# Ranks of the attention over three engines' later steps, and the first expert's gather above the jump

## The chip, the cores and the metric

One core of a Trainium2 chip runs the program. Its engines are TensorE (PE, with its weight loads as PEld), VectorE (DVE), ScalarE (ACT), GpSimd (POOL) and SyncE (SP), which issues most of the DMAs; POOL issues the indirect ones. Each engine has its own instruction queue and works in order; semaphores join them. Matrix products accumulate in PSUM, all else lies in SBUF. The metric is the device time of one execution in microseconds (us), as a median of several runs.

## The reference

Three stages stand one behind the other, on 3072 tokens of width 384. Cut to what is computed:

```python
def _attn_ref(r, k, v, w, u):                     # 4 batches, 8 heads, 768 tokens, 48 wide
    for t in range(S):
        cur = np.einsum('bhd,bhe->bhde', u[None] * kt, vt)
        y[:, :, t] = np.einsum('bhd,bhde->bhe', rt, state + cur)
        state = w[None, :, :, None] * state + np.einsum('bhd,bhe->bhde', kt, vt)

def _moe_ref(x, w_gate, w1, w2):                  # 8 experts, 384 -> 1024 -> 384
    logits = x @ w_gate
    expert_idx = np.argmax(logits, axis=1)        # one expert for each token
    probs = np.exp(logits - logits.max(-1, keepdims=True))
    probs /= probs.sum(-1, keepdims=True) + 1e-09
    for e in range(E):
        mask = expert_idx == e
        ye = np.maximum(x[mask] @ w1[e], 0.0) @ w2[e]
        out[mask] = gate_w[mask, None] * ye       # gate_w: the chosen expert's probs

def _moe2_ref(x, w_in, w_out):                    # 384 -> 2048 -> 384
    h = x @ w_in
    return (h - np.tanh(h)) @ w_out
```

## The kernel before, in words

**Attention** (to about 145 us). The sequence is cut into chunks of 128 tokens, six for each of the four batches: 24 steps, chunk by chunk, so that four steps belong to one chunk. The loop over `n` in `manual_schedule` writes the work of all engines in one order by hand, and every engine takes its part of it in that order. Around step `n`, SP loads the input of step `n + 3` (`load`, tiles n and t), POOL makes rk, rku, kh (L318, L324, L333, the keys and receptances scaled for a coming step) and sw (L382, the state decayed), DVE makes dt (L338), t (L313), am (L360) and Sc (L383), ACT makes am's diagonal (L345), copies y (L413) and the state Sb (L395), and PE the products between. Seven steps late, `xout_t` (L541) turns the output round through PE, `xout_g` scales it by the gate on ACT (xs, L548) and SP stores it in DRAM (xd, L550); the SP queue holds that store ahead of the load that follows it.

**Gate and ranks.** `at_step(n, first, fn)` calls `fn(c)` for chunk `c` at the step that lies `first` behind the chunk's start, counted so that it falls on one step in four. `logits`, `logits2`, `gate` find the expert of each token (OH, one-hot), `rank_mm` counts on PE how many earlier tokens went there. `rank_sel` (L483 on) makes of it the token's rank (RK), the tile hs and the row lo within the tile, by comparing with thr, and from them one-hot arrays: `ohh` (L495) and `ol` (L511) on DVE, `hv` (L500) and the tile part of `rh` (L504) on POOL, and the row part of `rh` (L509) on ACT, for the chunk before the last on POOL (L507). `idx_mm` (L520) multiplies `ol` by `rh` on PE, and the sum over chunks (`idf`, L529) is the list of tokens sorted by expert. All of `rank_sel` stands in one step, the *rank step*, and `idx_mm` in the next.

**Head and jump.** The first 256 tokens of expert 0 can be known after four chunks; their product with that expert's weights, the *head* (`head1`, `head2` for f from 0 to 7, nine matmuls each), fills PE around the end of the attention. `EARLY` of the head2 stand before the jump `tc.If(fr > 0)` (L837), whose body is skipped here and redoes the head in another case. Behind the jump, the casting of the list (L856) and `first_gather` (two indirect DMAs of 128 rows, L595) fetch the other tokens of the first block; `first_trans(kk)` for kk from 0 to 2 turns them on PE (L601), ACT casts (L602) and DVE subtracts (L603). The small DVE operations of `order()` are handed out between the heads as `steps`.

**Experts** (159 to 380 us): 64 blocks, eight for each expert. In block `i` the kernel runs `mm1(i)` (L1043) and `mm2(i)` (L1068). `gather(e + 2)` stands at the sixth block of expert e: three or four indirect DMAs (L1019) on POOL; `xg_trans` turns them three to five blocks of the next expert on. `refill` loads weights by SP (L76) and splits them on ACT (L84) and on DVE or POOL (L85). **Second FFN** (380 us to the end): `nm1` and `nm2` (L1295, L1343).

Of the kernel before, what the change touches and what calls it, by code (L numbers as in the profile page):

```python
# [30 lines left out]
def rwkv_moe_moe_kernel(ctx: ExitStack, tc: tile.TileContext, rk_t, rkv, pk, u, wp1, wp2, out):  # L31


    nc = tc.nc
# [382 lines left out]
    e8p, s4p = sm[:, 32:32 + E], sm[:, 32 + E:32 + 2 * E]  # L417
    scp = sm[:, 64:64 + B * E].rearrange("p (b e) -> p b e", e=E)
# [64 lines left out]
    def rank_sel(c):  # L483
        rk = sm[:, 192:192 + 8 * B].rearrange("p (b e) -> p b e", e=E)
        pr = gp.tile([P, B, E], F32, tag="pr", name="pr")
        nc.vector.tensor_tensor(out=pr, in0=rk, in1=OH[:, c], op=ALU.mult)
        rank = RK[:, c]
        nc.vector.tensor_reduce(out=rank, in_=pr, axis=AX.X, op=ALU.add)
        ge = gp.tile([P, B, 4], F32, tag="ge", name="ge")
        nc.vector.tensor_tensor(out=ge, in0=bc(rank.unsqueeze(2), [P, B, 4]),  # L490
                                in1=thr.unsqueeze(1).to_broadcast([P, B, 4]), op=ALU.is_ge)
        hs = gp.tile([P, B], F32, tag="hs", name="hs")
        nc.vector.tensor_reduce(out=hs, in_=ge, axis=AX.X, op=ALU.add)
        ohh = gp.tile([P, B, 4], F16, tag="ohh", name="ohh")
        nc.vector.tensor_tensor(out=ohh, in0=bc(hs.unsqueeze(2), [P, B, 4]),  # L495
                                in1=q1.unsqueeze(1).to_broadcast([P, B, 4]), op=ALU.is_equal)
        lo = gp.tile([P, B], F32, tag="lo", name="lo")
        nc.vector.scalar_tensor_tensor(out=lo, in0=hs, scalar=float(-P), in1=rank, op0=ALU.mult, op1=ALU.add)
# [11 lines left out]
        ol = gp.tile([P, B, P], F16, tag="ol", name="ol")  # L510
        nc.vector.tensor_tensor(out=ol, in0=iotaf.unsqueeze(1).to_broadcast([P, B, P]), in1=bc(lo.unsqueeze(2), [P, B, P]),  # L511
                                op=ALU.is_equal)
        st["ol", c], st["rh", c] = ol, rh
# [109 lines left out]
    def by_token():  # L623

        with tc.tile_pool(name="slow", bufs=1) as sp:
# [10 lines left out]
            for c in range(C):  # L636
# [33 lines left out]
                rank_sel(c)  # L670
                idx_mm(c)
# [4 lines left out]
    with tc.manual_schedule():  # L676
# [39 lines left out]
        LAG = 7  # L716
        LOADS = {1: (0, 0), 3: (0, 1), 5: (1, 0), 7: (1, 1), 9: (2, 0), 11: (2, 1), NN - 1: (3, 0)}
# [3 lines left out]
        for n in range(NN + 1):  # L721
# [54 lines left out]
            if n < NN:  # L776
                at_step(n, 5, idx_mm)
# [17 lines left out]
        L = C - 1  # L795
        EARLY = 2
# [17 lines left out]
        logits(L)  # L814
        xout_t(NN - 6)
# [15 lines left out]
        rank_sel(L)  # L831
        head1(1)
        head1(2)
        idx_mm(L)
        for f in range(EARLY):
            head2(f)
        with tc.If(fr > 0, label="slow"):  # L837
# [85 lines left out]
        for f in range(CH1):  # L923
# [7 lines left out]
            if 0 <= f - (CH1 - 3 - KD) < KD:  # L931
                first_trans(f - (CH1 - 3 - KD))
# [269 lines left out]
    with tc.manual_schedule():  # L1202
# [8 lines left out]
        for i in range(NC1):  # L1211
# [19 lines left out]
            if f == CH1 - 3 and e + 2 < E:  # L1231
                gather(e + 2)
# [228 lines left out]
```

## Time and profile before

| what | us |
|---|---|
| median of 3 runs (lowest, highest) | 792.38 (791.72, 793.81) |
| the profiled execution's own time | 790.21 |
| its span, first to last instruction | 786.5 |
| PE busy | 763.5 (97%) |
| PE's weight loads busy | 696.9 (89%) |
| DVE busy | 637.8 (81%) |
| ACT busy | 524.7 (67%) |
| POOL busy | 450.8 (57%) |

The mean granted clock of TensorE is 0.997 of full speed. Busy times are averages over three very different stages, and each stage has to be read by itself: the windows cut the span, the timeline lists the instructions of an engine in order with the idle time ahead of each and what ended it, and the waits add such times up by line.

### The profile page before, as it was taken

How to read it: one execution, taken by the hardware profiler on the slowest of the kernel's cores; microseconds unless marked ns; L12 is line 12 of the kernel's file. 1: busy time of each engine (PE TensorE's matmuls, PEld its weight loads, DVE VectorE, ACT ScalarE, POOL GpSimd, SP SyncE). 2: the span in 40 equal slices, each digit the busy share in tenths (PEclk: the TensorE clock that was granted, in tenths of full speed). 3: DMA queues.
4: the chain of work that ended last, by engine and by line, in shares of the span. 5: the costliest groups of instructions: out<-in, count | busy, mean ns of one | idle time of the engine just before them, and what ended most of it. 6: DMA issues, size and time to landing. Idle time of an engine off the chain costs nothing.

```text
span 786.5 us, 14413 instructions
## 1 busy us (share of the span) xinstructions
PE 763.5 (97%) x5052; PEld 696.9 (89%) x5052; DVE 637.8 (81%) x1124; ACT 524.7 (67%) x1135; POOL 450.8 (57%) x438
## 2 busy tenths in 40 slices
PE   7799999999999999999999999999999999999997
PEld 7578887898899989999899889989989988998887
DVE  6799888678798868994598888888888888888893
ACT  8789888454545545545687777777776677777871
POOL 6999995257668668665265443534435354353533
PEclk9999999999999999999999999999999999999999
DMA  7989973267798979974200000000001000000100
GB/s 216 261 234 281 249 241 115 86 193 233 200 241 257 276 233 280 261 241 134 80 1 1 1 30 11 2 11 31 0 2 41 1 0 21 21 1 0 42 1 40
DMA packets 34972, 89.82 MB, mean 114 GB/s; under 512 B 5690, under 2 KB 13022, under 8 KB 34896
## 3 DMA queue, kind: packets, MB, share of 16 engines
q1 hardware_dynamic: 30704, 78.87, 34.4%
q0 software_dynamic: 4192, 9.99, 4.3%
q8 instruction: 41, 0.67, 0.4%
q14 instruction: 35, 0.29, 0.1%
HBM read 73.10 MB, written 15.74 MB: 113 GB/s over the span
## 4 chain that ended last, share of the span: by engine, by line
PE 50%; issue 2%; ACT 1%; POOL 1%; POOLq 0%
PE h L1295 25%; PE o L1343 23%; PE y L1068 1%; PE hps L1043 1%; POOL out_dram L1356 0%; PE o L1295 0%; POOL g L1332 0%; POOLq L1402 0%; POOL xb L1332 0%; ACT mk L1305 0%; ACT s L1303 0%; POOLq L1456 0%; ACT xb L1331 0%; ACT z L1299 0%; ACT t L1301 0%
## 5 line engine op out<-in xcount | busy, mean ns | idle before, releaser
L1332 POOL TENSOR_TENSOR g<-t,g 128x512 fp32r<-128x512 f32 x93 | 120.3, 1294 | 178.2 <-ACT g L1331 126.7
L1295 PE MATMUL h<-xb,ring 128*128 128x512 f32 x855 | 213.6, 395 | 0.0
L1343 PE MATMUL o<-ring,g 128*128 128x384 f32 x1116 | 209.4, 336 | 0.0
L1343 PEld LDWEIGHTS o<-ring,g 128*128 128x128 f32 x1116 | 196.1, 188 | 8.2
L1295 PEld LDWEIGHTS h<-xb,ring 128*128 128x128 f32 x855 | 159.7, 188 | 30.5
L85 POOL TENSOR_TENSOR ring<-stg,ring 128x384 fp32r<-128x384 f32 x102 | 104.5, 1049 | 55.7 <-ACT ring L84 48.3
L1299 ACT ACTIVATE z<-h 128x512 f32<-128x512 f32 x95 | 56.9, 599 | 96.5 <-PE h L1295 96.5
L1068 PE MATMUL y<-h,ring 128*128 128x256 f32 (+7 forms) x576 | 114.0, 342 | 0.0
L1043 PE MATMUL hps<-xt,ring 128*128 128x472 f32 (+6 forms) x504 | 105.8, 354 | 1.4 <-DVE h L1047 1.3
L1068 PEld LDWEIGHTS y<-h,ring 128*128 128x128 f32 x576 | 101.4, 188 | 3.2
L1311 DVE TENSOR_TENSOR t<-t,h 128x512 f32<-128x512 f32 x95 | 65.0, 684 | 41.8 <-ACT t L1301 41.5
L1043 PEld LDWEIGHTS hps<-xt,ring 128*128 128x128 f32 x504 | 90.5, 188 | 5.4 <-DVE h L1047 1.4
L84 ACT CAST ring<-stg 128x384 fp32r<-128x384 f32 x152 | 70.4, 513 | 18.7 <-DMA stg<-in_wp_dram 18.2
L1316 DVE COPY_PREDICATED t<-mk,h 128x512 f32<-128x512 uint32 x95 | 71.5, 752 | 10.5 <-DVE h L1314 0.9
L1313 DVE SCALAR_TENSOR_TENSOR h<-s,h 128x512 f32<-128x512 f32 x95 | 66.2, 696 | 9.9
L1046 ACT ACTIVATE h<-hps 128x256 fp32r<-128x256 f32 (+7 forms) x64 | 32.0, 501 | 56.9 <-PE hps L1043 56.6
L1303 ACT ACTIVATE s<-z,gb 128x512 f32<-128x512 f32 x96 | 69.6, 725 | 0.0
L1305 ACT ACTIVATE mk<-z,gt 128x512 f32<-128x512 f32 x96 | 69.3, 722 | 0.0
L1314 DVE SCALAR_TENSOR_TENSOR h<-z,h 128x512 f32<-128x512 f32 x95 | 66.1, 696 | 3.3
L1312 DVE TENSOR_TENSOR h<-h,z 128x512 f32<-128x512 f32 x95 | 65.8, 692 | 0.0
L1331 ACT CAST g<-t 128x512 fp32r<-128x512 f32 x93 | 57.6, 619 | 8.5 <-DVE t L1316 6.4
L345 ACT ACTIVATE am<-ident,dt 128x128 f32<-128x128 f32 x192 | 58.6, 390 | 3.1 <-DVE dt L338 3.0
(246 smaller groups left out, 1095.2 us busy)
## 6 DMA issues: line engine op xcount, KB each, us to landing
stg<-in_wp_dram SPq DMA_DIRECT2D x64, 384.0 KB, 4.9
n<-in_rkv_dram SPq DMA_DIRECT2D x24, 576.0 KB, 7.2
d<-in_wp_dram SPq DMA_DIRECT2D x32, 384.0 KB, 6.0
t<-in_rk_t_dram SPq DMA_DIRECT2D x48, 192.0 KB, 7.5
wdec<-dcf SPq DMA_DIRECT2D x32, 192.0 KB, 5.5
xd<-xs SPq DMA_DIRECT2D x24, 192.0 KB, 3.1
stg<-wdec SPq DMA_DIRECT2D x12, 384.0 KB, 4.1
wl<-wdec SPq DMA_DIRECT2D x2, 768.0 KB, 5.1
```

The costliest lines, as they stand in the source:

```text
L84: nc.scalar.copy(out=dst[:, 0, sl], in_=of)
L85: eng.tensor_tensor(out=dst[:, 1, sl], in0=of, in1=dst[:, 0, sl].bitcast(F32), op=ALU.subtract)
L1043: nc.tensor.matmul(ps, lhsT=wf(a, kk), rhs=xt[e][b][:, kk, :], start=(n == 0), stop=(n == 8))
L1068: nc.tensor.matmul(yps[d], lhsT=wf(a)[:, d * P:(d + 1) * P], rhs=h2[:, b, :], start=(f == 0 and n == 0), stop=(f == CH1 - 1 and n == 2))
L1295: nc.tensor.matmul(ps, lhsT=wf(a, kk), rhs=xb[j][:, b, kk, :], start=(n == 0), stop=(n == 8))
L1303: nc.scalar.activation(out=s, in_=z, func=ACTF.Square, scale=G_K ** 0.5, bias=gb)
L1305: nc.scalar.activation(out=mk, in_=z, func=ACTF.Relu, scale=-1.0, bias=gt2)
L1313: nc.vector.scalar_tensor_tensor(out=ps, in0=s, scalar=G_K * G_D, in1=ps, op0=ALU.add, op1=ALU.mult)
L1314: nc.vector.scalar_tensor_tensor(out=ps, in0=z, scalar=G_A, in1=ps, op0=ALU.subtract, op1=ALU.mult)
L1316: nc.vector.copy_predicated(out=t, mask=mk.bitcast(U32), data=ps)
L1332: nc.gpsimd.tensor_tensor(out=g[:, 1, :], in0=ww, in1=g[:, 0, :].bitcast(F32), op=ALU.subtract)
L1343: nc.tensor.matmul(ops[q], lhsT=gg[i][:, b, q * P:(q + 1) * P], rhs=wf(a), start=(f == 0 and n == 0), stop=(f == CH2 - 1 and n == 2))
```

## The change

It moves work between steps, and three small arrays to another memory:

- `rank_sel` is cut in pieces. `rank_of` (rank, ge, hs) stays in the rank step; `rank_in` (lo, ohh, ol) comes one step later; `rank_q` (hv and the tile part of rh, on POOL), `rank_row` (the row part, now on ACT for every chunk) and `idx_mm` come one step after that. What needs the list for the head comes one step later with it.
- thr is copied to PSUM (thp), and hs and lo are made there (hsp, lop).
- `first`, the cast of the list and the first gather, stands above the jump and in the skipped body; EARLY is 1, not 2; `first_trans` stands at f = 4, 5, 6, not 2, 3, 4.
- `gather(e + 2)` is spread over three blocks: two parts at f = 5, one at 6, one at 7.

```diff
+    thp, hsp, lop = sm[:, 48:52], sm[:, 52:56], sm[:, 56:60]
...
     def rank_sel(c):
+        rank_of(c)
+        rank_in(c)
+
+    def rank_of(c):
...
-                                in1=thr.unsqueeze(1).to_broadcast([P, B, 4]), op=ALU.is_ge)
-        hs = gp.tile([P, B], F32, tag="hs", name="hs")
-        nc.vector.tensor_reduce(out=hs, in_=ge, axis=AX.X, op=ALU.add)
+                                in1=thp.unsqueeze(1).to_broadcast([P, B, 4]), op=ALU.is_ge)
+        nc.vector.tensor_reduce(out=hsp, in_=ge, axis=AX.X, op=ALU.add)
+
+    def rank_in(c):
+        nc.vector.scalar_tensor_tensor(out=lop, in0=hsp, scalar=float(-P), in1=RK[:, c], op0=ALU.mult, op1=ALU.add)
...
+        nc.vector.tensor_tensor(out=ol, in0=iotaf.unsqueeze(1).to_broadcast([P, B, P]),
+                                in1=bc(lop.unsqueeze(2), [P, B, P]), op=ALU.is_equal)
+    def rank_q(c):
...
-        if c == C - 2:
-            nc.gpsimd.tensor_scalar(out=rh[:, :, 1, :], in0=hv, scalar1=pid, scalar2=None, op0=ALU.mult)
-        else:
-            nc.scalar.activation(out=rh[:, :, 1, :], in_=hv, func=ACTF.Copy, scale=pid)
+    def rank_row(c):
+        nc.scalar.activation(out=st["rh", c][:, :, 1, :], in_=st.pop(("hv", c)), func=ACTF.Copy, scale=pid)
...
             at_step(n, 2, logits)
+            at_step(n, 6, rank_q)
...
                 outp(n - 1)
+                at_step(n, 6, rank_row)
...
+            at_step(n, 6, idx_mm)
...
-            at_step(n, 4, rank_sel)
+            at_step(n, 4, rank_of)
+            at_step(n, 5, rank_in)
...
-                at_step(n, 5, idx_mm)
...
+                nc.vector.tensor_copy(out=thp, in_=thr)
...
-        EARLY = 2
+        EARLY = 1
+        rank_q(L - 1)
+
+        def first():
+            nc.vector.tensor_copy(out=idx[:, 0:4], in_=idf[:, 0:4])
+            first_gather()
...
         logits(L)
+        rank_row(L - 1)
...
         rank_sel(L)
+        rank_q(L)
+        rank_row(L)
         head1(1)
         head1(2)
         idx_mm(L)
+        first()
         for f in range(EARLY):
             head2(f)
         with tc.If(fr > 0, label="slow"):
...
-            if 0 <= f - (CH1 - 3 - KD) < KD:
-                first_trans(f - (CH1 - 3 - KD))
+            if 0 <= f - (CH1 - 1 - KD) < KD:
+                first_trans(f - (CH1 - 1 - KD))
...
-            if f == CH1 - 3 and e + 2 < E:
-                gather(e + 2)
+            if f >= CH1 - 3 and e + 2 < E:
+                gather(e + 2, ((0, 1), (2,), (3,))[f - (CH1 - 3)])
```

POOL's queue in the attention, from a rank step (- before, + after; L512 and L516 are `hv` and the tile part of `rh` in the changed file):

```order
-L500 TENSOR_TENSOR hv<-OH,ohh 128x128
-L504 TENSOR_TENSOR rh<-hv,tileid 128x4x32
 L382 TENSOR_TENSOR sw<-Sc_140,pq 128x192
 L318 TENSOR_TENSOR rk<-n_130 128x384
 L324 TENSOR_TENSOR rku<-rk,ub 128x384
 L333 TENSOR_TENSOR kh<-n_130,KT 128x384
+L512 TENSOR_TENSOR hv<-OH,ohh 128x128
+L516 TENSOR_TENSOR rh<-hv,tileid 128x4x32
 L382 TENSOR_TENSOR sw<-Sc_141,pq 128x192
```

`hv` and `rh` move behind four operations, to the place just ahead of the next sw.

ACT's queue over the same steps, before (L509 is the row part of `rh`, L548 xs, L429 the copy of the logits):

```order
L345 ACTIVATE am<-ident,dt 128x128 x8
L509 ACTIVATE rh<-hv,pid 128x4x32
L413 COPY y<-yh_157 128x2x128
L413 COPY y<-yh_158 128x2x128
L395 COPY Sb_147<-Sc_143 64x4x48 x2
L548 ACTIVATE xs<-Xps,gt 128x384
L345 ACTIVATE am<-ident,dt 128x128 x8
L429 COPY lt<-lps 128x512
```

And after (L521 is the row part, L552 xs, L430 the copy of the logits):

```order
L413 COPY y<-yh_157 128x2x128
L413 COPY y<-yh_158 128x2x128
L395 COPY Sb_147<-Sc_143 64x4x48 x2
L552 ACTIVATE xs<-Xps,gt 128x384
L345 ACTIVATE am<-ident,dt 128x128 x8
L430 COPY lt<-lps 128x512
L413 COPY y<-yh_157 128x2x128
L413 COPY y<-yh_158 128x2x128
L521 ACTIVATE rh<-hv,pid 128x4x32
L395 COPY Sb_144<-Sc_140 64x4x48 x2
L552 ACTIVATE xs<-Xps,gt 128x384
```

The row stands one step later than it did, behind that step's copies of y and ahead of its Sb and xs.

POOL's queue at the jump, after (L599 is the first gather, L574 that of the head; before, the two rows L599 stand behind the branch):

```order
L574 DMA n_134<-xd,idxh 128x384
L574 DMA n_130<-xd,idxh 128x384
L512 TENSOR_TENSOR hv<-OH,ohh 128x128
L516 TENSOR_TENSOR rh<-hv,tileid 128x4x32
L815 TENSOR_LOAD flag
L512 TENSOR_TENSOR hv<-OH,ohh 128x128
L516 TENSOR_TENSOR rh<-hv,tileid 128x4x32
L599 DMA n_131<-xd,idx 128x384
L599 DMA n_132<-xd,idx 128x384
L856 COMPARE_AND_BRANCH
```

The gather has left the far side of the branch and stands behind the last chunk's `rh`.

PE's queue behind the jump, before (L610 is head1, L620 head2, L601 the transposes of the first gather):

```order
L837 UNCONDITIONAL_BRANCH x2
L1456 BRANCH_PREFETCH_HINT
L610 MATMUL hp_2199<-f_2214,ring_70 128x256 x6
L610 MATMUL hp_2199<-f_2210,ring_70 128x256 x3
L610 MATMUL hp_2200<-f_2214,ring_71 128x256 x6
L610 MATMUL hp_2200<-f_2210,ring_71 128x256 x3
L620 MATMUL yh_157<-f_2213,ring_70 128x256 x3
L620 MATMUL yh_158<-f_2213,ring_70 128x256 x3
L620 MATMUL yh_159<-f_2213,ring_70 128x256 x3
L610 MATMUL hp_2199<-f_2214,ring_71 128x256 x6
L610 MATMUL hp_2199<-f_2210,ring_71 128x256 x3
L601 MATMUL fx<-ident,n_131 128x128
```

And after, the piece with the first transposes (L614 is head1, L624 head2, L605 the transposes):

```order
L614 MATMUL hp_2190<-f_2204,ring_72 128x256 x6
L614 MATMUL hp_2190<-f_2200,ring_72 128x256 x3
L624 MATMUL yh_157<-f_2202,ring_71 128x256 x3
L624 MATMUL yh_158<-f_2202,ring_71 128x256 x3
L624 MATMUL yh_159<-f_2202,ring_71 128x256 x3
L614 MATMUL hp_2189<-f_2204,ring_72 128x256 x6
L614 MATMUL hp_2189<-f_2200,ring_72 128x256 x3
L605 MATMUL fx<-ident,n_131 128x128
L605 MATMUL fx<-ident,n_132 128x128
```

Before, 36 matmuls lie between the branch and the first transpose, now 81: that one stands behind the last head1.

## Rows read from the trace of the kernel before

**Rows 1.** Windows: us, then each engine's busy time and instructions, clock, DMA share, GB/s.

```profile
60.00:80.00 20.00, 19.53 (x306) 17.32 (x300) 18.21 (x39) 18.09 (x58) 19.50 (x19) 1.00 0.99 276
...
380.00:787.00 407.00, 401.67 (x2018) 362.28 (x2016) 331.31 (x487) 288.87 (x522) 174.77 (x143) 1.00 0.03 13
```

**Rows 2.** Timeline of POOL, 50 to 110 us: start, length, operation, idle before.

```profile
50.70 1.00 POOL L318 TENSOR_TENSOR rk<-n 128x384 f32<-128x384 f32 x1
...
70.32 1.99 POOL L318 TENSOR_TENSOR rk<-n 128x384 f32<-128x384 f32 x1
...
74.45 0.40 POOL L500 TENSOR_TENSOR hv<-OH,ohh 128x128 f16<-128x128 f16 x1
...
80.09 1.49 POOL L382 TENSOR_TENSOR sw<-Sc,pq 128x192 f32<-128x192 f32 x1
81.55 1.01 POOL L318 TENSOR_TENSOR rk<-n 128x384 f32<-128x384 f32 x1
...
86.02 1.01 POOL L318 TENSOR_TENSOR rk<-n 128x384 f32<-128x384 f32 x1
...
89.50 1.99 POOL L318 TENSOR_TENSOR rk<-n 128x384 f32<-128x384 f32 x1
...
108.91 1.01 POOL L318 TENSOR_TENSOR rk<-n 128x384 f32<-128x384 f32 x1
```

**Rows 3.** Instructions by form, 40 to 120 us: count, busy us, mean ns.

```profile
L511 DVE TENSOR_TENSOR ol<-iotaf,lo 128x512 f16<-128x512 f32 x4 | 3.2, 806 | 0.1
```

**Rows 4.** Waits, 40 to 120 us: total us, times, longest.

```profile
ACT rh L509 <- POOL hv L500: 8.2, 4, 2.3
PEld Xps L541 <- ACT xs L548: 4.0, 4, 1.1
...
POOL hv L500 <- DVE lo L498: 1.6, 3, 0.8
...
PE sm L520 <- POOL rh L504: 1.1, 2, 0.7
```

**Rows 5.** Timeline of ACT and DVE, 79.5 to 83 us.

```profile
79.74 0.64 ACT L413 COPY y<-yh 128x256 f32<-128x256 f32 x2
...
81.19 1.36 DVE L360 COPY_PREDICATED am<-mlt,A 128x512 f32<-128x512 uint32 x2
```

**Rows 6.** Timeline of SP, 62 to 104 us.

```profile
82.07 0.38 SPq L236 DMA_DIRECT2D n<-in_rkv_dram  x1
```

**Rows 7.** The tile n, 76 to 92 us: its loads, from issue to landing.

```profile
DMA to landing us min/median/max: 5.3/6.6/7.2
```

**Rows 8.** The page's DMA issues: count, KB, median us to landing.

```profile
xd<-xs SPq DMA_DIRECT2D x24, 192.0 KB, 3.1
```

**Rows 9.** Timeline around the jump, 131 to 160 us.

```profile
135.59 5.70 SPq L550 DMA_DIRECT2D xd<-xs  x6
...
144.97 0.19 DVE L529 TENSOR_TENSOR idf<-idf,sm 128x32 f32<-128x32 f32 x1 [1.70 <-PEq L837]
...
145.23 2.39 PE L610 MATMUL hp<-f,ring 128*128 128x256 f32 x18 [0.39 <-DVE idf L529]
...
145.63 1.03 POOL L595 DMA_INDIRECT n<-xd,idx  x1 [3.62 <-DVE key L861]
...
150.72 0.72 PE L601 MATMUL fx<-ident,n 128*128 128x128 f32 x2 [0.94 <-PE hp L610]
...
159.24 1.00 PE L1043 MATMUL hps<-ring,ring 128*128 128x256 f32 x7
```

**Rows 10.** Timelines of POOL, SP, ACT and PE's weight loads, 267 to 292 us.

```profile
268.74 1.00 POOL L1019 DMA_INDIRECT xg<-xd,idx  x1 [0.30 <-issue]
...
277.75 0.34 SPq L76 DMA_DIRECT2D stg<-in_wp_dram  x1
...
288.03 0.93 ACT L84 CAST ring<-stg 128x384 fp32r<-128x384 f32 x2 [4.11 <-DMA stg<-in_wp_dram]
...
290.57 1.61 PEld L1043 LDWEIGHTS hps<-xt,ring 128*128 128x128 f32 x9 [1.39 <-DVE h L1047]
```

More of the change, by code (lines that the diff above doesn't have):

```diff
@@ L490, in rank_sel @@
         nc.vector.tensor_tensor(out=ge, in0=bc(rank.unsqueeze(2), [P, B, 4]),
-                                in1=thr.unsqueeze(1).to_broadcast([P, B, 4]), op=ALU.is_ge)
-        hs = gp.tile([P, B], F32, tag="hs", name="hs")
-        nc.vector.tensor_reduce(out=hs, in_=ge, axis=AX.X, op=ALU.add)
+                                in1=thp.unsqueeze(1).to_broadcast([P, B, 4]), op=ALU.is_ge)
+        nc.vector.tensor_reduce(out=hsp, in_=ge, axis=AX.X, op=ALU.add)
+    def rank_in(c):
+        nc.vector.scalar_tensor_tensor(out=lop, in0=hsp, scalar=float(-P), in1=RK[:, c], op0=ALU.mult, op1=ALU.add)
         ohh = gp.tile([P, B, 4], F16, tag="ohh", name="ohh")
-        nc.vector.tensor_tensor(out=ohh, in0=bc(hs.unsqueeze(2), [P, B, 4]),
+        nc.vector.tensor_tensor(out=ohh, in0=bc(hsp.unsqueeze(2), [P, B, 4]),
                                 in1=q1.unsqueeze(1).to_broadcast([P, B, 4]), op=ALU.is_equal)
-        lo = gp.tile([P, B], F32, tag="lo", name="lo")
-        nc.vector.scalar_tensor_tensor(out=lo, in0=hs, scalar=float(-P), in1=rank, op0=ALU.mult, op1=ALU.add)
+        ol = gp.tile([P, B, P], F16, tag="ol", name="ol")
+        nc.vector.tensor_tensor(out=ol, in0=iotaf.unsqueeze(1).to_broadcast([P, B, P]),
+                                in1=bc(lop.unsqueeze(2), [P, B, P]), op=ALU.is_equal)
+        st["ohh", c], st["ol", c] = ohh, ol
+    def rank_q(c):
+        ohh = st.pop(("ohh", c))
         hv = gp.tile([P, B, E * 4], F16, tag="hv", name="hv")
@@ L505, in rank_sel @@
                                 in1=bc(tileid[:, c * B:(c + 1) * B].unsqueeze(2), [P, B, E * 4]), op=ALU.mult)
-        if c == C - 2:
-            nc.gpsimd.tensor_scalar(out=rh[:, :, 1, :], in0=hv, scalar1=pid, scalar2=None, op0=ALU.mult)
-        else:
-            nc.scalar.activation(out=rh[:, :, 1, :], in_=hv, func=ACTF.Copy, scale=pid)
[L510 to L513, printed above, removed]
+        st["hv", c], st["rh", c] = hv, rh
+    def rank_row(c):
+        nc.scalar.activation(out=st["rh", c][:, :, 1, :], in_=st.pop(("hv", c)), func=ACTF.Copy, scale=pid)
     def idx_mm(c):
@@ L521, in idx_mm @@
                                  start=(b == 0 and h == 0), stop=(b == B - 1 and h == 1))
-        if c < C - 1:
-            idx_add(c)
-    def idx_add(c):
         if c == 0:
@@ L670, in by_token @@
                 rank_sel(c)
+                rank_q(c)
+                rank_row(c)
                 idx_mm(c)
@@ L716, in rwkv_moe_moe_kernel @@
         LAG = 7
+        L = C - 1
         LOADS = {1: (0, 0), 3: (0, 1), 5: (1, 0), 7: (1, 1), 9: (2, 0), 11: (2, 1), NN - 1: (3, 0)}
@@ L772, in rwkv_moe_moe_kernel @@
             at_step(n, 4, rank_mm)
-            at_step(n, 4, rank_sel)
+            at_step(n, 4, rank_of)
+            at_step(n, 5, rank_in)
             if n == H0 * B + 3:
                 head_end()
-            if n < NN:
-                at_step(n, 5, idx_mm)
             if n == NN - 2:
@@ L793, in rwkv_moe_moe_kernel @@
                 w_split(*SPLITS[n])
-        L = C - 1
-        EARLY = 2
+        EARLY = 1
[3 more added lines that the diff above has]
+            first_gather()
         for q in range(2):
@@ L849, in rwkv_moe_moe_kernel @@
             counts()
+            first()
             for f in range(EARLY):
                 head2(f)
-        idx_add(L)
         def order():
-            nc.vector.tensor_copy(out=idx[:, 0:4], in_=idf[:, 0:4])
-            first_gather()
             cnt0 = gp.tile([P, E], F32, tag="cnt0", name="cnt0", bufs=1)
@@ L1014, in rwkv_moe_moe_kernel, with gather @@
     xg, xt = {}, {0: xt0}
-    def gather(e):
+    def gather(e, parts=range(4)):
         for q, n in enumerate(rows[e]):
+            if q not in parts:
+                continue
             t = xgp.tile([P, DM], F32, tag="xg", name="xg")
```

## The prediction

> **What bounds the kernel now.** I read the busy time by windows first [rows 1], whose columns are the five engines and DMA. From 380 us on TensorE (PE) is busy all but the ends of the window, and the change touches nothing there: 400 of the 786 us can't move. In the attention (60 to 80 us) four engines are at 18 to 19.5 of 20 us and the DMA share is 0.99, so it is bound by several things at once, and the question is what its period is made of. GpSimd's (POOL's) timeline [rows 2] shows it: four steps of the attention belong to one chunk, and one of the four carries the chunk's ranks. The operation rk opens a step. From rank step to rank step it is 50.70 to 70.32, to 89.50, to 108.91: 19.62, 19.18 and 19.41 us. A step without ranks is 81.55 to 86.02, 4.47 us. POOL is back to back there, but not with short work: sw (L382) takes 1.49 at 80.09 where VectorE's (DVE's) L313 runs beside it. L313 reads two SBUF arrays of 1024 elements in each partition; so POOL and L313 take turns, and POOL with L313 is the chain of the step.
>
> One period so has 4 x 4.47 = 17.88 of it, hv with 0.40 [rows 2], rh of the same size and 0.1 between them: 18.8. The measured periods are 0.4 to 0.8 above. In them lies `ol` (L511, two SBUF arrays, 0.81 on average [rows 3]), and POOL's wait for `lo`, 1.6 in three ranks [rows 4].
>
> The list of waits [rows 4] then tells what the ranks cost the others: ScalarE (ACT) stands 8.2 us in four waits before the rank row rh (L509), and behind it the scaled output xs comes late, for which PE stands 4.0 us in four waits. Of a period of 19.4, PE so stands 1.0 for xs, and 0.55 for rh where it does (1.1 in two): it needs 17.9, less than POOL's 18.8 (its busy 19.53 in [rows 1] has modelled ends, and its weight loads fill only 17.32). Its waits are mostly slack that falls there; what POOL gives back is what counts, until the ranks of the last chunks, where sw has gone and PE's own waits count.
>
> **The ranks.** *Removed*: ACT's wait in the rank step, and `ol`'s turn at the shared read: the arrays thr, hs and lo move to PSUM, so that ge, ohh, ol and lo read one SBUF array each. The rows for a DVE operation with a PSUM input beside POOL are rk at 81.55, 1.01 [rows 2], and L360 from 81.19 to 82.55 beside it [rows 5]: neither is stretched. So I take `ol` off the port in full. A read from PSUM could itself be slower or faster; L360 does two of 512 elements in 1.36, 0.68 each, so `ol` would be at 0.7 in place of 0.81, and ge, ohh and lo, with 4 and 16 elements, change by nothing that counts. The added copy of thr is one such small operation at step 3, early in the attention: nothing, at most 0.2.
>
> *Moved*: `hv` and the tile part of rh stand one POOL step later, after kh and before sw, when `ohh` is long there. POOL's wait for `lo` goes. But hv then stands where sw stands now, just when L313 holds the port: sw at 80.09 took 1.49 [rows 2], where its size, half that of rk, would take half of rk's 1.01, and the same 1.0 will fall on hv; sw behind it then runs short. So POOL's sum is the same, 18.8, and its order differs. Three periods: (19.62 - 18.8) + (19.18 - 18.8) + (19.41 - 18.8) = 1.8 us. This is the first term.
>
> The row part of rh goes on ACT after the two copies y of that later step. hv would end near 80.09 + 1.4 = 81.5, y ends at 80.38 [rows 5]: ACT still waits, about 1.1 per chunk, in place of 2.05 (8.2 / 4). Behind it on ACT stand Sb, xs and eight am, and behind xs on SyncE's queue (SP) the store of the step and the load of the input for the step three later. The next Xps on PE uses the other buffer, so PE doesn't stand. The load does count: today's store of that step is followed by the load at 82.07 [rows 6], which lands after 6.6, the median [rows 7], at 88.7, and rk reads it at 89.50: 0.8 of slack. The store gets the row (0.4) and the wait of 1.1 ahead of it, and less of what ACT waited in the rank step (2.05 and the row itself, of which ACT has caught up perhaps half by then, 1.2); with a period that wants to be 0.6 shorter the load comes 0.4 + 1.1 - 1.2 + 0.6 = 0.9 later against its reader, on 0.8 of slack. I take 0.2, more than this 0.1, for the other two periods, whose slack I know less: 3 x 0.2 = 0.6 lost. Bounds: none (1.8 stays) to all of it (0).
>
> Behind 108.91 there is no sw, and PE is the limit: there its fourth wait for xs (some 1.0 of the 4.0) can close. The row of the chunk before the last goes from POOL and ACT to ACT, ahead of two xs that the store waits for; it costs nothing if they have room, at most its own 0.4. So the ranks: 1.8 - 0.6 + 1.0 = 2.2 us gained; from 0 (loads eat it) to 5.1 (PE's waits for xs, 4.0, and for rh, 1.1 [rows 4], all close).
>
> The Trainium skill, "SBUF — State Buffer", section "Who interferes with whom", says that a DVE instruction with two SBUF inputs contends with a GpSimd instruction that reads SBUF, that the one that issues first blocks the other for the whole instruction, and that with at most one SBUF input there is no contention. The stretched sw and the unstretched rk [rows 2] agree. By its issue order it speaks against the place of hv, as the third case below has it from the rows; by its rule for one input `ol` costs POOL nothing, which is the first term.
>
> **The first gather.** [Rows 9] show the jump today: `idf` waits 1.70 for PE's branch, PE goes on at 145.23 after 0.39, and POOL issues its first gather only at 145.63, after 3.62 of standing. The transposes of the gathered rows (L601) are placed 36 matmuls later, and PE stands 0.94 before them. Now the cast of the indices and both gathers stand above the jump. They need idx_mm(L), which is done by then, and the last store of xd (issued by 135.59 + 5.70 = 141.3 [rows 9], landing 3.1 later [rows 8]): the gather may start near 144.3, so it is only 1.3 earlier, but the transposes also stand 45 matmuls later: 45 x 0.133 (2.39 / 18) = 6 us. They come near 155 by PE; the rows, which are there at 150.7 today, by 150: the wait goes, 0.94, and with it what the second of the transposes waits for its half, some 0.2: 1.1. The nine matmuls of head2 that EARLY takes from above the jump to below are the same work: nothing. At the jump PE waits for DVE and ACT, not for POOL, so POOL's gathers don't hold it; DVE has `idf` (0.19) and a cast of its size more ahead of it, beside nine matmuls. What is late next: after the last transpose only nine matmuls (1.24) stand before the first expert's L1043, and in them ACT's cast (L602) and DVE's L603 must end, on a DVE that also works off the small operations of the order. I take 0.1 for that: gain 1.0. Bounds: 1.5 gained (1.1 and the jump's 0.39) to 0.1 lost (1.1 less a wait of 1.2 at L1043, if L603 ends only that far behind the nine matmuls that should hide it).
>
> **The gathers of the experts.** Today four stand in a row, the first at 268.74 [rows 10], 1.0 each and 0.3 of issue: 5.2. While POOL issues them, its splits of weights (L85) wait; SP issues its next weight load only at 277.75, ACT at last waits 4.11 for one, h comes late, and PE with its weight loads stands 1.39 at 290.57 [rows 10]. With two, one and one, POOL is held 2.6 at a time. I take somewhat under half of the 1.4: 0.6 gained. Bounds: 1.4, to 0.5 lost: the last part comes two blocks later, each 3.4 us ((380 - 159) / 64), but the transposes that need it are three blocks, 10 us, behind, and a POOL split late by one part (1.3) could cost part of that anywhere.
>
> **The sum.** 2.2 + 1.0 + 0.6 = 3.8 less, on the profiled execution's own 790.21: 786.4. That execution lies 2.17 below the median of the runs, 792.38, so in runs I expect 792.38 - 3.8 = 788.6.
>
> **The rivals.**
> - *The loads bound the attention.* For it: DMA at 0.99 from 60 to 80 and 0.8 of slack [rows 1, 6, 7]. Against it: other steps' loads have more, and the share includes weights that stop early. Then the ranks give only the 0.6 to 1.0 of the tail; in all 0.6 + 1.0 + 0.6 = 2.2: 790.2.
> - *PE's waits all close.* For it: they are named after the moved operations [rows 4]. Against it: POOL's 18.8. Then 5.1 + 1.0 + 0.6 = 6.7: 785.7.
> - *The new place of hv is worse (slower).* hv behind L313, as sw at 80.09. It decides if ACT stands over 2 us before the row: then xs, the store and the load are 1.5 late or more against 0.8 of slack, POOL stands 1.6 per period at rk, 4.8 in three, less 1.8 and less 1.0 for the first gather: +2.0, 794.4. Against it: 1.1 from the rows.
> - *PSUM doesn't take `ol` off the port.* hv no longer runs beside it, but another of POOL's operations would be held for 0.7 to 0.8: 0.4 x 3 of the first term goes and 0.1 more of ohh, 1.3, so that 3.8 - 1.3 = 2.5 are gained: 789.9. Against it: rk beside L360.
>
> **How the numbers follow.** The forecast 0.45; loads 0.19; PE's waits 0.14; PSUM without use 0.13; the new place worse 0.09. A difference under 0.3% (2.4 us) can't be told from none here. Faster by more: the forecast and PE's waits for the most part, half of the PSUM case and a third of the loads': 0.42 + 0.14 + 0.06 + 0.05 = 0.67. Slower by more than 0.3% (above 794.8): half of the third case, and with less the bounds of the gathers in the loads' case: 0.06. The rest 0.27. The range: from PE's waits with the jump's gap closed too (785.7 - 0.5 = 785.2) to no change, 792.4; what lies outside is some 0.06 below and 0.12 above.
>
> **What would show it.** Right: rank steps 18.8 to 19.0 apart on POOL; ACT's wait before the row near 1.1 and in the later step; no wait for `lo`; hv about 1.4 long and the sw behind it 0.5; `ol` at 0.7 with POOL's operation beside it at 1.0; PE's wait for xs gone; no wait before the transposes of the first gather, and L1043 right behind; the stall near 290 half or gone. Wrong: rk waiting for a DMA (loads); a wait over 2 us before the row (the slower case); PE back to back over a whole period of 17.9 (PE's waits); POOL stretched beside `ol`; a wait of PE at the first L1043, or a new stall in the experts behind a later gather.

## The result, and the profile after

The changed kernel takes 784.58 us (median of 6 runs, 782.29 to 785.62) against 792.38 (790.58 to 793.81) beside it: a ratio of 0.9900 [0.9878, 0.9921]. That is 7.8 us faster, twice the forecast 3.8, and 0.6 below the range. The profiled execution is a long one of its runs: own time 785.56, span 783.7, granted clock 0.994. So the spans of the two profiles differ by only 2.8, and 1.9 more lies outside them: own time less span was 3.7 before and is 1.9 now.

The windows of the profile after, over the stretches of [rows 1] and then from rank step to rank step and on to the jump's first head matmul:

```profile
60.00:80.00 20.00, 19.83 (x290) 17.56 (x290) 18.43 (x43) 18.57 (x61) 17.98 (x20) 1.00 1.03 287
380.00:787.00 407.00, 398.97 (x2006) 360.09 (x2004) 331.17 (x487) 287.81 (x520) 174.52 (x143) 0.99 0.03 12
...
53.05:71.82 18.77, 17.85 (x268) 15.50 (x267) 17.36 (x38) 16.72 (x55) 18.12 (x19) 1.00 1.01 279
71.82:90.72 18.90, 18.73 (x282) 16.45 (x284) 16.89 (x38) 17.49 (x57) 17.14 (x19) 1.00 1.00 274
90.72:109.39 18.67, 18.44 (x280) 16.10 (x278) 16.94 (x38) 17.13 (x55) 18.17 (x20) 1.00 0.93 260
109.39:143.27 33.88, 33.28 (x390) 27.98 (x387) 27.79 (x81) 26.91 (x78) 17.14 (x19) 1.00 0.51 156
```

The same four stretches of the kernel before, which the prediction had not cut this way:

```profile
50.70:70.32 19.62, 18.24 (x269) 15.92 (x267) 17.86 (x39) 16.83 (x55) 18.53 (x20) 1.00 0.89 255
70.32:89.50 19.18, 18.71 (x284) 16.56 (x282) 17.42 (x38) 17.27 (x56) 18.68 (x20) 1.00 0.98 279
89.50:108.91 19.41, 18.58 (x278) 16.36 (x276) 16.86 (x37) 16.94 (x55) 18.84 (x20) 1.00 0.88 242
108.91:145.23 36.32, 34.32 (x395) 28.89 (x392) 29.15 (x81) 26.40 (x76) 19.40 (x19) 1.00 0.44 141
```

The rank steps are now 18.77, 18.90 and 18.67 apart, 1.87 less in three periods; PE's busy time in the second and third period is 18.4 to 18.7 in both kernels, so PE has little left to give there. The stretch behind them is 2.44 shorter. Some 1.0 of it (PE busy 33.28, not 34.32) belongs to the nine matmuls of head2 that stand below the jump now.

POOL's timeline in the first of these periods, to set beside [rows 2]:

```profile
53.05 1.00 POOL L318 TENSOR_TENSOR rk<-n 128x384 f32<-128x384 f32 x1 [1.32 <-DMA n<-in_rkv_dram]
...
58.45 1.87 POOL L324 TENSOR_TENSOR rku<-rk,ub 128x384 f32<-128x384 f32 x1
...
61.33 0.40 POOL L512 TENSOR_TENSOR hv<-OH,ohh 128x128 f16<-128x128 f16 x1
...
62.16 0.52 POOL L382 TENSOR_TENSOR sw<-Sc,pq 128x192 f32<-128x192 f32 x1
```

And DVE's beside it:

```profile
57.72 1.74 DVE L313 TENSOR_TENSOR t<-t,PRK 128x1024 f32<-128x1024 f32 x1
...
61.16 0.68 DVE L505 TENSOR_TENSOR ol<-iotaf,sm 128x512 f16<-128x512 f32 x1
...
62.22 1.54 DVE L313 TENSOR_TENSOR t<-t,PRK 128x1024 f32<-128x1024 f32 x1
```

hv runs beside ol in 0.40: DVE's small operations of the rank stand ahead of L313, so L313 falls here on rku (1.87 at 58.45), not on hv. The waits from 40 to 120 us show what that does, beside [rows 4]:

```profile
ACT y L413 <- PE yh L408: 5.7, 12, 1.3
...
POOL rk L318 <- DMA n<-in_rkv_dram: 3.4, 4, 1.4
PEld Xps L545 <- ACT xs L552: 3.4, 4, 0.8
```

ACT's wait for hv (8.2 before) is gone in this profile; ACT now waits for PE. POOL waits for loads, 3.4 in four. The weight loads of Xps still wait 3.4 (4.0 before), yet PE has no wait there: those waits lie under matmuls.

At the jump, beside [rows 9]:

```profile
142.90 0.99 POOL L599 DMA_INDIRECT n<-xd,idx  x1 [2.12 <-DVE idx L809]
...
143.27 1.30 PE L614 MATMUL hp<-f,ring 128*128 128x256 f32 x9 [0.44 <-DVEq L856]
...
153.06 0.38 PE L605 MATMUL fx<-ident,n 128*128 128x128 f32 x2
...
157.30 1.93 PE L1062 MATMUL hps<-ring,ring 128*128 128x256 f32 x14 [0.22 <-DVE ring L607]
```

The gather issues 0.4 ahead of PE's first matmul behind the jump (0.4 behind it before), its transposes wait for nothing, and the first expert starts 0.22 late. In the experts the 1.39 near 290 [rows 10] is gone, and one shorter wait is new:

```profile
190.26 1.97 PE L1087 MATMUL y<-h,ring 128*128 128x472 f32 x8 [0.60 <-DVE h L1066]
```

### The profile page after: what moved, and what is told of

It is laid out like the page before. It is cut to its first block, busy times and chain, and to the rows that moved or that the text cites. A ratio compares the mean times of both kernels' runs of the same rounds, so it can differ in the third digit from the quotient of the medians.

```text
span 783.7 us, 14420 instructions
## 1 busy us (share of the span) xinstructions
PE 763.8 (97%) x5052; PEld 697.1 (89%) x5052; DVE 641.5 (82%) x1125; ACT 525.4 (67%) x1136; POOL 446.1 (57%) x437
## 4 chain that ended last, share of the span: by engine, by line
PE 50%; issue 2%; ACT 1%; POOL 1%; POOLq 0%
PE h L1314 25%; PE o L1362 23%; PE y L1087 1%; PE hps L1062 1%; POOL out_dram L1375 0%; PE o L1314 0%; POOL g L1351 0%; POOLq L1421 0%; POOL xb L1351 0%; ACT mk L1324 0%; ACT s L1322 0%; POOLq L1475 0%; ACT xb L1350 0%; ACT z L1318 0%; ACT t L1320 0%
## 5 line engine op out<-in xcount | busy, mean ns | idle before, releaser
L1062 PE MATMUL hps<-xt,ring 128*128 128x472 f32 (+6 forms) x504 | 105.6, 353 | 0.1
L1062 PEld LDWEIGHTS hps<-xt,ring 128*128 128x128 f32 x504 | 90.6, 188 | 3.7 <-DVEq L1201 0.4
```

Source lines behind the costliest of these rows:

```text
L1062: nc.tensor.matmul(ps, lhsT=wf(a, kk), rhs=xt[e][b][:, kk, :], start=(n == 0), stop=(n == 8))
```

## The experiments

Each set of kernels ran on one chip with the kernel before beside it. For every run the own time and the span are known, so the table splits each median; "before" is that of the same set. Spans of one kernel in one set differ by 2 to 9 us from run to run, so a difference of two median spans under about 1 us is not clear of noise.

| kernel | us | ratio [95%] | span (before) | outside |
|---|---|---|---|---|
| before again (r1) | 791.38 | 1.0003 [0.9990, 1.0017] | 787.4 (787.1) | 3.7 |
| ranks alone (r2) | 787.77 | 0.9962 [0.9949, 0.9975] | 784.0 (787.1) | 3.6 |
| first gather alone (r3) | 788.19 | 0.9967 [0.9954, 0.9979] | 786.4 (787.1) | 1.75 |
| spread alone (r4) | 790.15 | 0.9995 [0.9980, 1.0011] | 786.25 (787.1) | 3.9 |
| after again (r5) | 786.50 | 0.9944 [0.9930, 0.9958] | 784.4 (787.15) | 1.8 |
| code only (r6) | 789.03 | 0.9975 [0.9965, 0.9985] | 787.2 (787.15) | 1.7 |
| PSUM only (r7) | 790.24 | 0.9996 [0.9983, 1.0008] | 786.4 (787.15) | 3.7 |
| later steps only (r8) | 787.90 | 0.9971 [0.9949, 0.9994] | 784.4 (787.15) | 3.8 |
| after, third (r9) | 786.20 | 0.9949 [0.9929, 0.9968] | 784.0 (786.75) | 1.8 |
| ranks and first (r10) | 787.00 | 0.9948 [0.9928, 0.9968] | 785.15 (786.75) | 1.8 |
| ranks and spread (r11) | 786.65 | 0.9946 [0.9926, 0.9966] | 782.6 (786.75) | 3.8 |
| early load (r12) | 794.63 | 1.0046 [1.0028, 1.0064] | 792.75 (786.75) | 1.8 |
| transposes earlier (r13) | 784.55 | 0.9913 [0.9896, 0.9930] | 782.85 (788.1) | 1.7 |
| early load, later start (r14) | 788.17 | 0.9958 [0.9937, 0.9979] | 786.3 (788.1) | 2.0 |
| both (r15) | 784.61 | 0.9906 [0.9888, 0.9923] | 782.6 (788.1) | 1.8 |
| after, fourth (r16) | 785.96 | 0.9935 [0.9916, 0.9953] | 784.1 (788.1) | 1.8 |
| transposes earlier again (r17) | 783.22 | 0.9900 [0.9879, 0.9921] | 781.5 (787.7) | 1.8 |
| after, fifth (r18) | 783.71 | 0.9903 [0.9883, 0.9923] | 781.9 (787.7) | 1.8 |

**The parts alone.** r1 is the kernel before, unedited; r2 takes the ranks' part of the change alone; r3 the first gather's:

```diff
-        EARLY = 2
+        EARLY = 1
+        def first():
+            nc.vector.tensor_copy(out=idx[:, 0:4], in_=idf[:, 0:4])
+            first_gather()
...
-            if 0 <= f - (CH1 - 3 - KD) < KD:
-                first_trans(f - (CH1 - 3 - KD))
+            if 0 <= f - (CH1 - 1 - KD) < KD:
+                first_trans(f - (CH1 - 1 - KD))
```

and r4 the experts':

```diff
-            if f == CH1 - 3 and e + 2 < E:
-                gather(e + 2)
+            if f >= CH1 - 3 and e + 2 < E:
+                gather(e + 2, ((0, 1), (2,), (3,))[f - (CH1 - 3)])
```

> The kernel before, unchanged, beside itself. The two profiles differ by 2.8 us in span and 4.65 in own time, the medians by 7.8. Theory 1 (the profiles are a lucky run of before and an unlucky one of after, the work itself is 6 to 8 us shorter): spans of this kernel lie around 788 to 789 in most runs, against 780.6 to 783.1 of the changed kernel, and their own times near 792.4. Theory 2 (some 3 us of the 7.8 lie outside the span or are noise of the median): spans around 786.5 and own times 3 to 6 us above them.

> Only the change of the attention's ranks (PSUM arrays, the three steps, the row on ACT for every chunk); the gathers as before. Theory 1 (the ranks were mis-sized: PE's waits close with POOL's): 4.5 to 6 us less than before. Theory 2 (the ranks give the 2.2 of the forecast and the rest comes from the two gathers or from their sum): 1.5 to 3 us less.

> Only the first gather above the jump, EARLY at 1 and the later transposes; the ranks and the other gathers as before. Both profiles say that its stretch, from the jump to the first L1043, is 14.0 us in both with nine matmuls (1.1) more in it after. Theory 1: 0.9 to 1.2 less than before, no more. Theory 2 (it also frees something behind L1043): 2 or more.

> Only the experts' gathers spread over three blocks. The stretch from the first L1043 to the second FFN became 0.7 shorter in the profile (the stall of 1.3 near 290 gone, a new one of 0.6 at 182 to 190). Theory 1: 0.5 to 0.8 less than before. Theory 2 (the stall at 290 is larger in most runs than in the profiled one): 1.3 to 3 less.

Before again: no difference. The ranks give 3.1, all in the span. The first gather gives 2.6, of which 0.7 lies in the span (within noise) and 1.95 outside. The spread's 0.7 is not clear by its interval; in its profile PE has no wait left in the experts, neither 1.39 nor 0.6. r2's windows show where the 3.1 is:

```profile
49.72:69.61 19.89, 19.23 (x300) 16.86 (x296) 18.55 (x45) 18.03 (x58) 18.51 (x19) 1.00 0.85 250
69.61:88.15 18.54, 18.50 (x284) 16.24 (x278) 17.11 (x38) 17.27 (x56) 18.10 (x20) 1.00 0.91 273
88.15:106.82 18.67, 18.67 (x290) 16.42 (x284) 16.91 (x39) 17.52 (x57) 18.18 (x19) 1.00 0.88 258
106.82:141.59 34.77, 34.32 (x399) 29.06 (x396) 27.78 (x82) 26.93 (x78) 16.79 (x18) 1.00 0.48 150
```

Length less PE's busy time is 0.66, 0.04, 0 and 0.45, in the kernel before 1.38, 0.47, 0.83 and 2.0. PE's idle time closes, and PE's own 18.5 to 18.7 is what stops the gain in the second and third period. The first period is longer than before, 19.89: POOL stands 0.99 in it before hv, for ohh. So the three together are only 1.1 shorter. The stretch behind the periods is 1.55 shorter.

**The outside time.** It fell wherever the first gather had moved. Two theories: what stands above the jump does it, or only that the code behind the jump then lies elsewhere. r6 is the kernel before with instructions that never run in the body that the jump skips; nothing is left out of the computation. One small memset stands above the jump besides:

```diff
+            for q in range(23):
+                nc.scalar.copy(out=pad[:, 0:4], in_=pad[:, 4:8])
+            for q in range(29):
+                nc.vector.memset(pad[:, 0:4], 0.0)
+            for q in range(32):
+                nc.gpsimd.memset(pad[:, 0:4], 0.0)
+            for q in range(18):
+                nc.sync.dma_start(out=pad[:, 0:4], in_=xd[0:P, 0:4])
```

r7 takes the three PSUM arrays alone, with the ranks in one step as before; r8 the later steps with the three arrays in SBUF. r5, and later r9, r16 and r18, are the changed kernel unedited.

```diff
-        hs = gp.tile([P, B], F32, tag="hs", name="hs")
+        hs = hsp
...
-        lo = gp.tile([P, B], F32, tag="lo", name="lo")
+        lo = lop
```

> The changed kernel, unchanged, beside the kernel before. The three parts alone took 3.3 (ranks), 0.8 (first gather) and 1.0 (spread) off the span of 787.3, and the first gather 1.9 more off what lies outside the span (own time less span: 3.7 before, 1.75 with it). Theory 1 (the parts add up): span 782.2, own time 784.0, 6.5 to 7.2 under before. Theory 2 (they take from each other or help each other): outside 783 to 786.

> The kernel before, with 18 to 32 small instructions on ACT, DVE, POOL and SP in the body that the jump skips, and one small memset above it; no executed work is otherwise changed. Every engine's code behind the jump so lies about as far on as in the changed kernel. Theory 1 (what the first gather took off outside the span is only where the code lies: before, three instruction fetches of 8 KB run after the last instruction): span 787.2 as before, own time less span 1.7 in place of 3.7, so 788.9 to 789.3. Theory 2 (it comes from the moved gather itself): own time less span stays at 3.6 to 3.8, 790.8.

> Only thr, hs and lo in PSUM; all of the ranks in the steps of before. Theory 1 (the shared read bounds the attention, and `ol` held it for 0.7 to 0.8 in each of the four ranks): hv and rh at 0.40 beside `ol`, span 0.8 to 1.8 less. Theory 2 (what counts is ACT's wait for hv in the rank step, which stays): within 0.5 of before.

> Only the later steps of the ranks (the split, the row on ACT in the later step, idx_mm with it), with thr, hs and lo in SBUF as before. Theory 1 (ACT's wait and what it makes late is the whole gain): span 2.8 to 3.5 less than before. Theory 2 (the shared read is, `ol` still holds it): 0.8 to 2 less.

r6 has the span of the kernel before, 787.2, and the outside time of the changed one, 1.73 against 3.77: code that never runs is enough for it. The queue q14 carries instructions; its rows for the window from 700 to 800 us, first of before:

```profile
q14 instruction: 5, 0.04, 0.1%
```

and of r6:

```profile
q14 instruction: 2, 0.02, 0.1%
```

Of before's five packets, three of 8 KB start after the last instruction, at 787.4, 787.5 and 790.0 us, where the span is 786.5; in the profile after none does. The same holds in every profile: three such packets behind the last instruction where the first gather stands below the jump (before, r1, r2, r4, r7, r8, r11), none where it stands above, and none in r6. So the moved gather most likely acts by the place of its code, as r6 does. Which engine fetches them, and why the end waits for them, no row shows.

PSUM alone leaves the periods at 19.3 and moves the span by 0.75, within noise, which the time doesn't show. The later steps alone give 2.75 of the span. In r8 hv stands beside an ol with two SBUF arrays:

```profile
78.36 0.84 POOL L515 TENSOR_TENSOR hv<-OH,ohh 128x128 f16<-128x128 f16 x1
```

and its ol takes 884 ns on average, 677 in the changed kernel, where hv takes 0.40. So the turn-taking that `ol` caused is real, and PSUM removes it; of the ranks' gain the order carries most (2.75 of the span in r8, 3.1 in r2 on another chip). The Trainium skill, "SBUF — State Buffer", "Who interferes with whom", says that a DVE instruction with at most one SBUF input does not contend with GpSimd, outside the modes in which it reads one input through two ports, and that one with two SBUF inputs contends with a GpSimd instruction that reads SBUF. The traces agree with these four numbers. r5 gave only 4.9, and its profile a wait that the first did not have: 2.0 before the first L1062.

**The late cast, and loads.** r10 leaves out the spread, r11 the first gather. r12 issues each load ahead of the store that stood before it; in its first steps a load so goes over a tile that the state still reads, and the state of a chunk differs.

```diff
-            if n + 3 < NN:
+            if n < 2:
                 load(n + 3)
...
+                if n + 4 < NN:
+                    load(n + 4)
```

> The changed kernel once more. It was 7.8 under before in the first timing (spans 780.6 to 783.7) and 4.9 in the second (783.8 to 785.5). In both profiles POOL stands at rk for the input's landing, 3.4 and 2.2 us; in that of the ranks alone, where loads landed after 5.7 in place of 8.3, never. Theory 1 (the shorter attention is bound by the loads, whose speed differs by chip and time): span between 782 and 785, lower where the profile shows fewer waits of rk. Theory 2 (the parts hurt each other): span 784.4, 0.4 or more above that of the ranks alone with the first gather.

> The changed kernel without the spread gathers. Theory 1 (parts add): span 0.7 to 1.0 above that of the changed kernel in this series, with the wait of 1.3 of PE near 290 back. Theory 2 (the spread hurts where the ranks are faster): span the same or lower than the changed kernel's.

> The changed kernel without the moved first gather (gather below the jump, EARLY at 2, transposes at f = 2, 3, 4). Theory 1 (parts add): span 0.7 to 1.0 above the changed kernel, and 1.9 more outside the span, so 2.6 to 2.9 slower in all. Theory 2: span as the changed kernel's, 1.9 slower in all.

> The changed kernel with SP's load of the input for the step n + 4 placed in step n, behind that step's output products and ahead of the store of xs, in place of behind the store at the head of step n + 1. Same transfers. Theory 1 (rk waits for loads that stand behind the late store): waits of rk under 1 in the profile, span 1 to 2.5 less than the changed kernel. Theory 2 (DMA itself is full, its share is 1.0): waits and span as in the changed kernel.

These runs of one chip part the effects: from r11 to r9 the first gather makes the span 1.4 longer and takes 2.0 away outside. In r9 and r10 PE waits 2.0 and 2.1 at the first L1062; with r3's 0.7 shorter, where that wait was 0.2, 1.8 - 0.7 = 1.1 of that 1.4 is the wait. The spread, from r10 to r9, is worth 1.15 of the span, which is not clear of noise. r12 lost 4.0 against before: its start runs late (the fifth rk at 35.61, in r9 at 28.77), and its time can't be compared.

r13 places the transposes one f earlier; r14 is r12 with the first three loads left as they were, and later ones ahead by one step; r15 has both:

```diff
-            if 0 <= f - (CH1 - 1 - KD) < KD:
-                first_trans(f - (CH1 - 1 - KD))
+            if 0 <= f - (CH1 - 2 - KD) < KD:
+                first_trans(f - (CH1 - 2 - KD))
```

```diff
-            if n + 3 < NN:
+            if n < 3:
                 load(n + 3)
...
+                if n > 1 and n + 4 < NN:
+                    load(n + 4)
```

> The changed kernel with the transposes of the first gather one block earlier (f = 3, 4, 5 in place of 4, 5, 6). In the profiles of three of the four kernels with both the later ranks and the moved gather PE waits 2.0 to 2.1 for L607 at the first L1062 (0.2 in the first profile). Theory 1 (the transposes are now placed too near to their use, and what comes late there is paid in full): the wait gone, span 1 to 2 below the changed kernel's 784. Theory 2 (the delay holds PE too, wherever the transposes stand): span as the changed kernel's.

> The changed kernel with SP's load for step n + 4 in step n, ahead of that step's store of xs, from step 2 on; the first steps load as before, so that nothing reads a tile that was loaded over. Theory 1 (rk waits for loads that stand behind the late store): no wait of rk for a DMA in the profile from 40 us on, span 0.5 to 1.5 less than the changed kernel. Theory 2 (DMA itself is full): waits and span unchanged.

> The changed kernel with both edits, transposes at f = 3, 4, 5 and loads ahead of the store. If both first theories hold: 1.5 to 3.5 less than the changed kernel, span near 781.5, own time near 783.3.

> The changed kernel beside these three. If its profile has the wait of 2 at L1062, span 784 to 784.5 and own time 786.2 as in the last two series; without it 782.3 and 784.1.

The changed kernel on this chip (r16) has the wait:

```profile
154.09 0.38 PE L605 MATMUL fx<-ident,n 128*128 128x128 f32 x2
...
156.63 0.37 ACT L606 CAST ring<-fx 128x256 fp32r<-128x256 f32 x1 [3.05 <-PE yh L624]
157.04 0.42 DVE L607 TENSOR_TENSOR ring<-fx,ring 128x256 fp32r<-128x256 f32 x1 [1.66 <-ACT ring L606]
157.52 1.70 PE L1062 MATMUL hps<-ring,ring 128*128 128x256 f32 x12 [1.98 <-DVE ring L607]
```

The last transposes end by 154.5, but ACT's cast begins only at 156.63, and PE's nine matmuls run out. In the profile after, the same cast starts at 156.05, behind transposes that end at 156.01. In r13 the last transposes end at 153.23, the cast starts at 153.27, and DVE's half comes 1.2 behind the cast; the matmuls between transposes and first expert are twice as many, and just cover it:

```profile
154.82 0.42 DVE L607 TENSOR_TENSOR ring<-fx,ring 128x256 fp32r<-128x256 f32 x1
155.29 0.90 PEld L1062 LDWEIGHTS hps<-ring,ring 128*128 128x128 f32 x7
155.29 0.98 PE L1062 MATMUL hps<-ring,ring 128*128 128x256 f32 x6
```

r13 is 1.4 faster than r16 (784.55 against 785.96). The early loads did not help: r14 is 2.2 slower than r16 and r15 as fast as r13. In their profiles, both of the longest run of the kernel (794.15 and 790.24), rk's waits for loads up to the jump are 7.6 in five in r14 and 14.9 in eleven in r15, 5.3 in five in r16. Why, was not tried.

> The version with the transposes at f = 3, 4, 5 once more. Theory 1 (the wait of 2 us at the first L1062 is a cost of where the last transpose stands): no such wait in the profile, 1 to 2 under the changed kernel beside it. Theory 2 (its 1.4 in the last series was chance): within 0.5 of it.

> The changed kernel beside it. Theory 1: the wait of 2 at L1062 in the profile, span 783.8 to 784.6. Theory 2: as the version beside it.

On another chip the changed kernel has no such wait (r18), and the earlier transposes are worth only 0.5 (783.22 against 783.71). The wait stood in the profiles of three chips (r5; r9, r10, r12; r14, r16) and in none of two others (r3; r18): without it the changed kernel's span is 782.45 and 781.9, with it 784.4, 784.0 and 784.1.

The profiles on record say more of the late cast. It is not ACT's alone, and not of the changed kernel: on these three chips something holds ACT and SP in all twelve profiles (r5 to r16), and on the two others in none (r1 to r4, r17, r18). In r16 POOL begins the fourth of the experts' gathers (xg) at 154.68. From 155.42 to 156.56 no engine begins an instruction; then SP issues its next load, and ACT's cast begins at 156.63:

```profile
154.68 0.99 POOL L1038 DMA_INDIRECT xg<-xd,idx  x1 [0.30 <-issue]
156.56 0.94 SPq L76 DMA_DIRECT2D stg<-in_wp_dram  x2
```

In r7, with gather and transposes where they were before, ACT's copy of the head's output comes at 160.68, 2.1 behind that gather and 1.04 behind the head's last matmul; in r1, on a chip without the hold, 0.08 behind it:

```profile
158.55 0.99 POOL L1021 DMA_INDIRECT xg<-xd,idx  x1 [0.30 <-issue]
160.68 0.65 ACT L946 COPY Y<-yh 128x256 f32<-128x256 f32 x2 [3.79 <-SPq L71]
```

In all twelve ACT goes on 1.9 to 2.2 after the fourth gather has begun. In r6, which runs the work of the kernel before, nothing that PE needs falls into this time. In the changed kernel the last transposes end 0.2 ahead of that gather, so the first expert waits for the cast; r13's end 1.3 ahead of it. That the gather causes the hold was not tried, and why three chips have it and two do not stays open. The earlier transposes so beat the changed kernel where the hold is (r13 against r16), and can't be told from it where it is not (r17 against r18).

**The periods in the other profiles.** The three periods from rank step to rank step take 58.2 to 58.3 in before, r1 and r3, and 59.5 in r4 and r6. In the ten profiles with the whole change of the ranks and the loads in their old place they take 55.7 (r9) to 58.4 (r10), 57.4 on average. A period in which POOL doesn't wait takes 18.2 to 18.7. What varies is two waits. In the first period hv stands 1.0 for ohh in seven of the ten (r2, r5, r10, r11, r13, r16, r17), 2.95 in r18, and not at all in two (the profile after, r9). And rk stands 0 to 2.4 for loads in the three periods, 0.85 on average. In r18:

```profile
62.33 0.40 POOL L512 TENSOR_TENSOR hv<-OH,ohh 128x128 f16<-128x128 f16 x1 [2.95 <-DVE ohh L502]
```

In one period each of r5, r10, r11 and r17, L313 starts ahead of hv, and hv is as long as forecast. In r5:

```profile
97.69 1.54 DVE L313 TENSOR_TENSOR t<-t,PRK 128x1024 f32<-128x1024 f32 x1
98.11 1.38 POOL L512 TENSOR_TENSOR hv<-OH,ohh 128x128 f16<-128x128 f16 x1
99.53 0.40 ACT L521 ACTIVATE rh<-hv,pid 128x128 f16<-128x128 f16 x1 [0.95 <-POOL hv L512]
```

These four periods are no longer than the others, 18.2 to 18.5.

## Why the prediction was wrong

**The step that failed** is the first line of the sum: it was made on the own time 790.21 as if what lies around the span, 3.7, could not move. It moved by 2.0. r6 gets the same 2.0 from code that never runs, so it takes neither work nor a wait of the kernel; the first gather's cast, gathers and matmuls, which move code too, most likely act in the same way. In spans alone the five sets give 6.2 (taking 3.7 outside for the 792.38, whose spans I set at 788.7), 2.75, 2.75, 4.0 and 5.8: 4.3 on average, against the forecast 3.8. With the outside 2.0 it is 6.3. The second step is the tail of the ranks, put at 1.0 for PE's wait for xs: it gave 1.8 to 2.0, and PE waited only 0.15 for xs there.

**The ranks** were mis-sized in the tail. In the three periods the forecast net of loads was 1.8 - 0.6 = 1.2; the profiles give 1.9 in the first one and 1.3 on average (58.7 before, 57.4). That is in part luck. POOL's 18.8 without waits is right (18.2 to 18.7), and the loads' 0.6 is near the 0.85. But the forecast had no wait before hv, since `ohh` should be there long; hv stands 1.0 or more for it in the first period of eight profiles out of ten. And I had PE's need at 17.9, since I took the weight loads' waits for xs [rows 4] for idle time of PE. They lie under other matmuls, and 3.4 of the 4.0 are still there; PE's own waits in the three periods before are 1.4 for am, 1.1 for rh and 0.15 for xs, and it needs 18.4 to 18.7.

The tail gave 2.0 from rank step to the first expert's first matmul (50.33 before, 48.35 in r2; 1.8 against r1 on the same chip), not 1.0, and not by xs. Up to the jump PE's waits for am, the rank product, f and xs close together, and its idle time falls from 2.0 to 0.45. In all the ranks gave 3.1 against 2.2.

ACT's wait for hv, forecast at 1.1, is 0 in most periods, because L313 starts behind the rank's operations and stretches rku in place of hv. In the four periods where L313 is first, hv takes 1.38 and ACT waits 0.95 to 1.04, as forecast: the price was right, and which of POOL's operations pays it differs from period to period. `ol` at 0.68 (forecast 0.7) and the port are right, so the PSUM rival fell, though by itself PSUM gains next to nothing. The slower rival's sum left out the 0.6 of the spread; its sign, ACT over 2 us before the row, came nowhere in the ten profiles.

**The first gather**: 0.7 in the span, within noise, against 1.0, with transposes that wait for nothing, as forecast. But the case named as what is late next, a wait at the first expert, has 2.0 and not at most 1.2 on three chips, and on the one of them where the step was timed by itself (r9 against r11) it loses 1.4 in the span.

**The spread**: 0.6 forecast; 0.85 (r4) and 1.15 (r9 to r10) in the span, neither clear of noise. The stall near 290 went; 0.6 came at 190, where DVE's h (L1066) is late. It stands in the profiles with the spread and the ranks together, not in r4; what ties it to them was not tried.

**What stays open.** The parts, 3.1, 0.7, 0.85 and 2.0, make 6.6; the sets without the late cast gave 7.8 and 7.7, those with it, for which they make 4.6, gave 4.9, 4.4 and 5.8. About 1 us between sets is explained by nothing shown; the periods alone, 55.7 to 58.4, vary by more than that.

The rival of PE's waits (785.7) came nearest to the time, but not for its reason: it had PE's waits for xs all close.

## What to carry to other kernels

Read the own time less the span for both kernels, and when it moves, test it by never-executed code in a skipped body: a gain that such code gives too is not the edit's own, and another edit may lose it. An idle time of the weight loads is PE's only where a window over the same stretch shows PE idle, so take what an engine needs in a period from its own windows from step to step. Where a chain of two other engines must end behind a fixed number of matmuls, leave it more cover than one trace shows it to need: nine more cost nothing here, and r13 beat r16 by 1.4 us on the chip where the chain came late. Where a new place makes an operation wait for another engine, look at several profiles: the wait of hv for `ohh` is not in the first one.

## What the chip showed unexpectedly

Instruction packets started up to 3.5 us after the last instruction (790.0 against 786.5), and the end of the execution came 3.7 us behind the span with them, about 1.8 without. In single runs it was longer with the code in the better place too, up to 4.1 (r9); in r18's profile, where it was 3.3, one more packet, of 16 KB, started at 786.2, 2.3 behind the last instruction. A cast started 2.2 us behind the end of its transposes (156.63 after 154.47, r16), and the hold that delays it stood in all profiles of three chips and in none of two others. Between 76 and 92 us loads of one kind landed in 5.8 us (r2) and 6.9 us (the changed kernel) in median, and the start of the attention came with them: the tenth rk at 49.72 and 53.05.
